# A new step table, norm moments partly on GpSimd, and a split key-value eviction in a one-core transformer block

## The chip, the core and the metric

The kernel runs on one core of a Trainium2 chip. A core has TensorE (PE, matmuls, with a separate weight load, PEld), VectorE (DVE), ScalarE (ACT), GpSimd (POOL) and SyncE (SP, which here only issues DMAs). Each engine works through its own queue in order; semaphores hold an instruction until what it needs is there. The metric is the device time of one execution in microseconds, lower is better.

## What is computed

S = 2048 tokens, D = 448, 16 heads of 28, Fh = 896. All inputs are bf16.

```python
mod = silu(c) @ w_mod                       # six rows sa, ca, ga, sb, cb, gb of 448
h = layernorm(x) * (1 + ca) + sa
q, k, v = split(h @ wqkv)                   # 16 heads of 28
phi(u) = concat(softmax(u @ w_phi), softmax(-(u @ w_phi)))     # 56 features a head
kv = phi(k)^T @ v;  z = sum_s phi(k)
x = x + ga * (((phi(q) @ kv) / (phi(q) @ z + 1e-6)) @ wo)
h = layernorm(x) * (1 + cb) + sb
z = gelu(h @ w_in);  z1, z2 = z[:, :896], layernorm(z[:, 896:])
g = w_sp @ z2 + b_sp[:, None]               # 2048 x 2048 over the tokens
out = x + gb * ((z1 * g) @ w_out)
```

## The kernel before, in words

The fast path does everything on 16 token tiles of 128. (A general path stands behind a flag that the fast path computes; it isn't taken with these inputs.) Its stages, with the names of the steps:

- *Head.* wq and wk are transposed on PE (FTq, FTk, two halves each), copied out of PSUM (ETq, ETk), multiplied with the block-diagonal w_phi (PFq, PFk, four pieces each) and copied out again (EPq, EPk). The first layer norm's shift and scale are folded into the weights: csA and ccA form the columns on PE, esA and ecA evict them, SHq, SHk, SHv put the shift in as one more row of the weights, SCq, SCk, SCv scale the rows. The first token tiles get their statistics (l1s, l1e, l1r), are normalised (l1a) and transposed on PE (X, copied by XE); the others are transposed by DMA (T1). Steps du are warm-up matmuls on zeros.
- *Key stage.* For each tile i: kM (keys), kE and kF (exponential of plus and minus on ACT), kS (sums, DVE), kR (reciprocal), kP (normalise, on DVE or POOL), vM, vC (values, copied by ACT), kA (accumulate kv over the tiles in one bank). qM, qE, qF make the query features in eight steps that take 1024 columns each.
- *Between.* gr and ge form the gates ga and gb, wos and wts multiply them into wo and wout. KV masks the accumulated kv into a block-diagonal table KVbd, and a second small step writes its column 28. csB, ccB, esB, ecB, SHw, SCw fold the second norm into w_in (f_win).
- *Attention out.* Per tile nM (numerators), nX and nC, per pair nS (denominators), per tile nT (weights the numerators, DVE, f_t), nA (adds the two halves, into f_opad), T2 (DMA transpose), wM or wN (times wo; wN also adds x through a matmul with the identity), wR (evicts the new x with its row sum; on ACT after wN, on DVE with the addition of x after wM), wQ (row sum of squares).
- *Second norm.* l2R (moments from the two sums, four small DVE instructions), l2r (power -0.5, POOL), l2a (normalise), T3 (DMA transpose into f_hT).
- *z stage.* Per tile zM and zG (second half, gelu with row sum), zQ (squares), zR, zW and zN as l2R, l2r and l2a. yM and yG (first half) for each of four groups of 512 tokens and seven column pieces.
- *Token mixing.* w_sp is loaded transposed in 32 pieces (W), eight for each of four 512-column parts; part 0 has its own tile, parts 1 and 2 take the place of the query features, part 3 that of f_hT. gM sums over the 16 tiles, gG adds b_sp (bsp) and multiplies with z1, oM multiplies with wout, oE adds x, oD stores.

PSUM is cut by hand into five slots: A0, A1, A2 of two banks, B0, B1 of one. A step with @A1 waits until the readers of the step that had A1 before are done. The order in which the engines get all this is a table written out in the program, ORDER (line 482 and on): a word is a step with its arguments, after a slash the engine where there is a choice (V DVE, S ACT, G POOL, Y SP), after @ the PSUM slot. The loop at line 1092 issues the words one after the other, so every engine's queue is the table with the other engines' words left out. DMAs are words too (ld, T1 to T3, W, oD), nearly all in SP's queue; an SP word whose tile isn't ready holds back the words after it.

A scaling with one factor for each row is, on every engine but ACT, one instruction with a single multiplication (line 764):

```python
eng.tensor_scalar(out=out_, in0=in_, scalar1=sc, scalar2=None, op0=ALU.mult)
```

Lines that the prediction uses: L753, L758 shift rows; L764 scaling; L785, L801 head matmuls; L789, L791 copies; L819 l1a; L842 kM; L850 vM; L856 kS; L863 kP; L873 kA; L879, L881 KV; L890 qM; L895 qE and qF; L918 nM; L934 nT; L948 identity matmul of wN; L950 wM; L955, L957 wR; L970 to L973 moments; L976 powers; L990 zM; L1012 zN; L1018 yM; L1026 W; L1034 gM; L1047 oM; L1050 oE.

Of the kernel before, what the change touches and what calls it, by code (L numbers as in the profile page):

```python
# [482 lines left out]
ld:c/S ld:x0/Y ld:wq/S ld:x1/Y tbl ld:phi/Y m1/V m2a/G du:1@A2 ld:wk/Y ct@B0 ld:x2/Y du:8@A2 m2b/G ce:1 l1s:0 ld:wsa/Y ld:wca/Y ce:2 m3 ce:3 ld:x3/Y  # L483
l1e:0,1/G ce:4 FTq:1@B1 ld:wv/Y m4 l1s:1 ld:x4/Y FTq:0@B0 ETq:1/S du:7@A2 ETq:0/V l1r:0,1 ld:x5/Y bd/V l1e:1,2/V PFq:2@B0 l1a:0/V l1r:1,2 PFq:3@B1
PFq:1@A2 EPq:2/S ld:wo/Y FTk:0@A1 EPq:3/V EPq:1/S l1a:1/V X:0@B0 W:0,0 FTk:1@B1 l1s:2 XE:0/S X:1@A2 l1s:3 ETk:1/S PFq:0@B0 ETk:0/V l1e:2,4/G EPq:0/S
csA@A0 XE:1/S l1r:2,4 PFk:2@B0 esA PFk:3@B1 ld:wsb/S SHq@A2 EPk:3/V l1a:3/G ccA@A1 l1a:2/G X:3@B1 ecA PFk:0@A0 EPk:2/V SCq:0/S PFk:1@A1 SCq:1/V XE:3/S
X:2@B0 EPk:0/V du:6@A2 EPk:1/S l1s:4 SCq:3/S SHk@B1 l1s:5 XE:2/S SCq:2/S SHv@A2 SCk:2/V l1s:6 SCk:1/S qM:0@A1 SCk:0/S SCv:2/V SCk:3/V SCv:1/S SCv:3/V
l1s:7 SCv:0/S kM:0@B0 l1s:8 l1e:4,8/G qF:0 vM:0@B1 l1s:9 l1r:4,8 kE:0 vM:1@A2 l1s:10 kF:0 l1a:4/G vC:0 vM:2@B0 kS:0 vC:1 l1a:5/G vM:3@B1 qE:0 l1a:7/V
T1:4,6 kM:1@A2 kR:0 vC:2 l1a:6/V kP:0/G vC:3 l1s:11 kM:2@A1 T1:6,8 kE:1 l1s:12 kM:3@B0 kF:1 kF:2 l1s:13 qM:1@A2 l1e:8,12/G W:0,1 kE:3 kS:1 kF:3
l1r:8,12 kE:2 l1s:14 kA:0@A0 l1a:11/G qF:1 qM:2@A1 kS:2 l1a:10/G qE:1 W:0,7 kR:1 l1a:9/G kS:3 vM:4@B0 qF:2 l1a:8/G T1:10,12 vM:5@B1 kR:2 l1s:15 vC:4  # L490
kM:4@A2 qE:2 kP:1/V T1:8,10 kM:5@B0 kP:2/V kF:4 kR:3 kA:1@A0 kE:4 ld:wout/Y l1e:12,16/V kP:3/V kM:6@A1 ld:bsp/S l1r:12,16 W:0,3 kS:4 kE:5 kM:7@A2 kF:5
vC:5 kA:2@A0 kS:5 l1a:12/G kM:8@B0 kE:6 l1a:14/G kR:4 kF:6 kA:3@A0 kR:5 kP:4/V l1a:13/G vM:6@B1 ld:wmgb/Y kF:7 kS:6 kE:7 kA:4@A0 vC:6 vM:7@A1 kP:5/G
T1:12,14 kS:7 kE:8 vM:8@B1 kF:8 kR:6 vC:7 vM:9@A2 kS:8 l1a:15/G vC:8 ld:wmga/Y kA:5@A0 kP:6/V T1:14,16 kM:9@B0 vC:9 kR:7 kR:8 kA:6@A0 kP:7/V kE:9
kM:10@B1 kF:9 kP:8/V kA:7@A0 kS:9 kE:10 kM:11@B0 kF:10 kA:8@A0 kR:9 kF:11 kS:10 kP:9/G vM:10@B1 kE:11 vM:11@A2 kS:11 vC:10 ld:win1/S kM:12@B0 ld:wcb/Y
kR:10 vC:11 kR:11 kA:9@A0 kP:10/V kE:12 kM:13@B1 kP:11/V kF:12 kA:10@A0 kS:12 kF:13 kM:14@B0 kE:13 kA:11@A0 kR:12 kF:14 kS:13 kP:12/G vM:12@B1 kE:14
vM:13@A2 kS:14 vC:12 kM:15@B0 vC:13 kR:13 kR:14 kA:12@A0 kP:13/V kE:15 vM:14@B1 kP:14/V kF:15 kA:13@A0 scb kS:15 vC:14 vM:15@B0 kA:14@A0 kR:15 vC:15
kP:15/V gr:0@B1 kA:15@A0 ge:0 gr:1@B0 KV:0 wos:0/G ccB@B1 ge:1 wos:1/V qM:3@A2 wos:2/G ecB KV:1 wos:3/G csB@B0 qF:3 nM:0@A1 esB nM:1@A0 wts:1/G nX:0
SHw:3@B0 nC:0 ld:win0/Y nX:1 qE:3 nC:1 SHw:2@B1 nS:0 qM:4@A2 SCw:0,3/V SCw:2,1/S SCw:3,1/G nT:0 SCw:1,1/S nT:1 nA:0/G qM:5@A1 SCw:0,2/S qE:4 nA:1/G
# [654 lines left out]
```

## Time and profile before

| what | value |
|---|---|
| three runs, median (lowest to highest) | 266.71 us (266.34 to 267.99) |
| the profiled execution, its time | 266.28 us |
| its span, first to last instruction | 264.4 us |
| mean granted TensorE clock | 0.991 |
| PE, DVE, ACT, POOL busy | 254.1, 159.1, 113.2, 67.6 us |
| first wide matmul (qM:0) | 17.9 us |
| end of the last kA, with both gr | 56.0 us |
| end of zM:0 | 83.7 us |
| first gM | 138.5 us |
| last eviction starts, ends | 260.3, 260.95 us |

The profile shows one execution. Times in it count from the span's first instruction. Some 1.9 us of the execution lie outside the span. The duration of an instruction is longer than the distance to the next one where two follow each other, since their ends overlap: two exponentials of 448 columns (0.56 us each by the mean) take 0.98 together.

### The profile page before, as it was taken

What the parts mean: (1) busy time and instruction counts of PE and PEld (TensorE: products, weight loads), DVE (VectorE), ACT (ScalarE), POOL (GpSimd) and SP (SyncE); (2) the same over time, 40 slices, a digit from 0 to 9 for tenths busy, and PEclk for the clock granted to TensorE, in tenths of its full rate; (3) what the DMA queues carried; (4) which work ended last, traced back from release to release, by engine and by line L of the source; (5) the groups of instructions that cost most, each with busy time, mean ns of one, the idle gap of its engine ahead of it and who ended that gap; (6) DMA issues with size and microseconds to landing.
All of it is one profiled execution on the core that took longest, in us unless ns stands there. A gap on an engine that the chain in (4) does not pass through costs nothing.

```text
span 264.4 us, 4350 instructions
## 1 busy us (share of the span) xinstructions
PE 254.1 (96%) x1632; PEld 138.3 (52%) x1640; DVE 159.1 (60%) x389; ACT 113.2 (43%) x238; POOL 67.6 (26%) x93
## 2 busy tenths in 40 slices
...
PEclk9999999999979999999999999999999999999999
...
GB/s 183 280 240 117 157 240 250 281 5 13 106 147 174 119 82 41 160 160 42 185 186 29 0 0 0 2 0 0 0 5 35 97 180 132 0 0 30 24 36 80
DMA packets 68656, 25.23 MB, mean 95 GB/s; under 512 B 58129, under 2 KB 68498, under 8 KB 68626
## 3 DMA queue, kind: packets, MB, share of 16 engines
...
q10 hardware_dynamic: 1538, 2.15, 3.7%
q8 instruction: 15, 0.25, 0.4%
...
## 4 chain that ended last, share of the span: by engine, by line
PE 90%; ACT 3%; DVE 3%; DMA 2%; issue 1%; ACTq 0%; DVEq 0%
PE g_ps L1034 37%; PE z_ps L990 9%; PE z_ps L1018 9%; PE o_ps L1047 8%; PE q_ps L890 5%; PE k_ps L842 4%; PE x_ps L950 4%; PE v_ps L850 4%; PE kvacc L873 3%; PE num L918 2%; DMA f_wq_raw<-in_A_wqkv_dram 2%; DVE f_t L934 1%; PE tps L785 1%; PE sh_ps L758 1%; ACT f_Wq L762 1%; PE pf_ps L801 1%
## 5 line engine op out<-in xcount | busy, mean ns | idle before, releaser
L1034 PEld LDWEIGHTS <-f_z2n 128*128 128x128 bf16 x560 | 50.4, 98 | 47.6
L1040 DVE TENSOR_TENSOR f_gb<-g_ps,f_bsp 128x512 f32<-128x512 f32 (+2 forms) x35 | 20.4, 583 | 58.9 <-PE g_ps L1034 58.7
L1034 PE MATMUL g_ps<-f_Eq,f_z2n 128*128 128x512 bf16 x219 | 48.7, 379 | 0.3
L1021 ACT ACTIVATE f_z1T<-z_ps 128x512 bf16<-128x512 f32 x28 | 16.2, 595 | 71.0 <-PE z_ps L1018 71.0
L1018 PE MATMUL z_ps<-f_hT,f_win 113*128 113x512 bf16 (+1 forms) x112 | 26.4, 379 | 0.0
L990 PE MATMUL z_ps<-f_win,f_hT 112*128 112x448 bf16 (+1 forms) x128 | 26.1, 352 | 0.0
L1034 PE MATMUL g_ps<-f_hT,f_z2n 128*128 128x384 bf16 (+1 forms) x224 | 25.4, 272 | 0.0
L1034 PE MATMUL g_ps<-f_wsp,f_z2n 128*128 128x512 bf16 x109 | 24.5, 379 | 0.2
L1047 PE MATMUL o_ps<-f_wout,f_z1T 128*128 128x448 bf16 x112 | 22.8, 353 | 0.0
L1041 DVE TENSOR_TENSOR f_z1T<-f_gb,f_z1T 128x512 bf16<-128x512 f32 (+2 forms) x35 | 20.5, 585 | 1.9 <-ACT f_z1T L1021 0.5
L990 PEld LDWEIGHTS <-f_hT 112*128 112x128 bf16 (+1 forms) x128 | 12.3, 97 | 11.8
L856 DVE TENSOR_REDUCE f_ksum<-f_E 128x32 f32<-128x896 bf16 x16 | 16.8, 1067 | 0.8 <-ACT f_E L845 0.7
L1050 DVE TENSOR_TENSOR f_xpad<-o_ps,f_x 128x448 bf16<-128x448 f32 x16 | 9.3, 620 | 13.0 <-PE o_ps L1047 12.5
L1018 PEld LDWEIGHTS <-f_win 113*128 113x128 bf16 (+1 forms) x112 | 10.7, 97 | 12.3
L895 ACT ACTIVATE f_Eq<-q_ps 112x1024 bf16<-112x1024 f32 x16 | 16.0, 1034 | 2.7 <-PE q_ps L890 2.7
L934 DVE TENSOR_TENSOR f_t<-num,f_w 128x896 bf16<-128x896 f32 x16 | 16.7, 1084 | 0.2
L994 ACT ACTIVATE f_z2g<-z_ps 128x896 bf16<-128x896 f32 x16 | 14.6, 914 | 3.6 <-PE z_ps L990 3.5
L845 ACT ACTIVATE f_E<-k_ps 128x448 bf16<-128x448 f32 x32 | 15.4, 556 | 1.6 <-PE k_ps L842 0.9
L1047 PEld LDWEIGHTS <-f_z1T 128*128 128x128 bf16 x112 | 10.7, 98 | 9.4
L950 PE MATMUL x_ps<-f_wo,f_oT 112*128 112x448 bf16 x64 | 15.2, 367 | 0.0
L890 PE MATMUL q_ps<-f_hT,f_Wq 113*128 113x512 bf16 (+1 forms) x64 | 14.9, 378 | 0.0
L842 PE MATMUL k_ps<-f_Wk,f_hT 113*128 113x448 bf16 (+1 forms) x64 | 14.1, 352 | 0.0
...
## 6 DMA issues: line engine op xcount, KB each, us to landing
...
```

The lines of the kernel that those rows point to most:

```text
L842: nc.tensor.matmul(t[:, 0, 0:D], lhsT=hT[0:KR[m], i, m, :], rhs=Wk[0:KR[m], m, :], start=(m == 0), stop=(m == KC - 1))
L856: nc.vector.tensor_reduce(out=ksum[:, i], in_=Er[i % NR][:].rearrange("p s (c f h) -> p (s c) h f", c=4, h=HP), axis=AX.X, op=ALU.add)
L890: nc.tensor.matmul(t[:, u, :], lhsT=Wq[0:KR[m], m, cc * CB:cc * CB + P], rhs=hT[0:KR[m], 4 * st:4 * st + 4, m, :], start=(m == 0), stop=(m ...
L934: nc.vector.tensor_tensor(out=tr[i % 2][:], in0=numv(i)[:, :, :, 0:DH], in1=wr[i // 2 % 2][:, i % 2].unsqueeze(3).to_broadcast([P, 2, H, D ...
L950: nc.tensor.matmul(t[:, 0, 0:D], lhsT=oT[0:CB, i % 4, cc, :], rhs=wo_s[0:CB, cc, :], start=(cc == 0 and not with_x), stop=(cc == KC - 1))
L990: nc.tensor.matmul(t[:, hf, 0:D], lhsT=hT[0:KR[m], i, m, :], rhs=win_s[0:KR[m], m, FH + hf * D:FH + (hf + 1) * D], start=(m == 0), stop=(m ...
L1018: nc.tensor.matmul(t[:, 0, :], lhsT=win_s[0:KR[m], m, fc * P:(fc + 1) * P], rhs=hT[0:KR[m], 4 * st:4 * st + 4, m, :], start=(m == 0), stop ...
L1021: nc.scalar.activation(out=stage_b()["z1T"][:, fc, st * 512:(st + 1) * 512], in_=ps["y%d_%d" % (st, fc)][:, 0, :], func=ACT.Gelu_apprx_tanh)
L1034: nc.tensor.matmul(g[:, 0, 0:b - a], lhsT=later["z2n"][:, s_, fc * P:(fc + 1) * P], rhs=wspT[t][:, s_, a:b], start=(s_ == 0), stop=(s_ == ...
L1040: nc.vector.tensor_tensor(out=gb, in0=ps["G%d_%d" % (ch, fc)][:, 0, 0:b - a], in1=bsp[:, t * TCHF + a:t * TCHF + b], op=ALU.add)
L1041: nc.vector.tensor_tensor(out=z, in0=gb, in1=z, op=ALU.mult)
L1047: nc.tensor.matmul(ps["o" + str(t)][:, 0, 0:D], lhsT=later["z1T"][:, fc, t * P:(t + 1) * P], rhs=wout_s[:, fc, :], start=(fc == 0), stop=( ...
```

## The change

There are five parts.

1. ORDER is another table: the same steps, but in another order, some on other engines and other PSUM slots. In numbers: wN stands 4 times instead of 9 (the others are wM); wR is on DVE 12 times instead of 7; kP on POOL 6 times instead of 4; l1a on POOL 14 times instead of 12; l2a on POOL 15 times instead of 7; zN on POOL 5 times instead of 3; SCw on POOL 5 times instead of 2 and on DVE no more; wts on DVE 5 times instead of 1; warm-up matmuls 20 instead of 22; loads on ACT's queue 3 instead of 5. Before the first gM stand 20 yM words (24 before) and 24 W words (17 before).
2. moments takes an engine. On POOL it is five instructions, on DVE four as before. Three of the eight l2R and four of the eight zR are on POOL.
3. A scaling on POOL adds 0.0 and then multiplies, in one instruction.
4. KV is split: the masking of one half stays on DVE, that of the other is four ACT copies with the mask's column as scale (a float copy of the mask is made at the start); the small step for column 28 is a word of its own, KZ, on DVE.
5. A step dm (small matmuls on zeros) is defined, and the table doesn't use it.

The diff of the functions:

```diff
+        nc.vector.tensor_copy(out=maskf[:], in_=mask[:])
...
     def scale_on(eng, out_, in_, sc):
         if eng is nc.scalar:
             nc.scalar.activation(out=out_, in_=in_, func=ACT.Copy, scale=sc)
+        elif eng is nc.gpsimd:
+            eng.tensor_scalar(out=out_, in0=in_, scalar1=0.0, scalar2=sc, op0=ALU.add, op1=ALU.mult)
...
-    def KV(s):
+    def KV(s, eng):
         kvv = ps["kv"][0:CB, s, 0:464].rearrange("p (c h d) -> p c h d", c=4, h=HP)
-        nc.vector.tensor_tensor(out=KVbd[0:CB, s, :, :, 0:29], in0=kvv,
-                                in1=mask[0:CB].unsqueeze(1).unsqueeze(3).to_broadcast([CB, 4, HP, 29]), op=ALU.mult)
+        if eng is nc.scalar:
+            for h in range(HP):
+                nc.scalar.activation(out=KVbd[0:CB, s, :, h, 0:29], in_=kvv[:, :, h, :], func=ACT.Copy, scale=maskf[0:CB, h:h + 1])
+        else:
+            nc.vector.tensor_tensor(out=KVbd[0:CB, s, :, :, 0:29], in0=kvv,
+                                    in1=mask[0:CB].unsqueeze(1).unsqueeze(3).to_broadcast([CB, 4, HP, 29]), op=ALU.mult)
+
+    def KZ(s):
+        kvv = ps["kv"][0:CB, s, 0:464].rearrange("p (c h d) -> p c h d", c=4, h=HP)
         nc.vector.scalar_tensor_tensor(out=KVbd[0:CB, s, :, :, 28], in0=kvv[:, :, :, 28], scalar=0.5e-6,
...
-    def moments(a, b, t1, t2, n, nm, v):
-        nc.vector.tensor_scalar(out=nm[:, a:b], in0=t1[:, a:b], scalar1=-1.0 / n, scalar2=None, op0=ALU.mult)
-        nc.vector.tensor_tensor(out=sq[:, a:b], in0=nm[:, a:b], in1=nm[:, a:b], op=ALU.mult)
-        nc.vector.scalar_tensor_tensor(out=v[:, a:b], in0=t2[:, a:b], scalar=1.0 / n, in1=sq[:, a:b], op0=ALU.mult, op1=ALU.subtract)
-        nc.vector.tensor_scalar(out=v[:, a:b], in0=v[:, a:b], scalar1=0.0, scalar2=LN_EPS, op0=ALU.max, op1=ALU.add)
+    def moments(a, b, eng, t1, t2, n, nm, v):
+        eng.tensor_scalar(out=nm[:, a:b], in0=t1[:, a:b], scalar1=-1.0 / n, scalar2=None, op0=ALU.mult)
+        eng.tensor_tensor(out=sq[:, a:b], in0=nm[:, a:b], in1=nm[:, a:b], op=ALU.mult)
+        if eng is nc.gpsimd:
+            eng.tensor_scalar(out=v[:, a:b], in0=t2[:, a:b], scalar1=1.0 / n, scalar2=None, op0=ALU.mult)
+            eng.tensor_tensor(out=v[:, a:b], in0=v[:, a:b], in1=sq[:, a:b], op=ALU.subtract)
+        else:
+            eng.scalar_tensor_tensor(out=v[:, a:b], in0=t2[:, a:b], scalar=1.0 / n, in1=sq[:, a:b], op0=ALU.mult, op1=ALU.subtract)
+        eng.tensor_scalar(out=v[:, a:b], in0=v[:, a:b], scalar1=0.0, scalar2=LN_EPS, op0=ALU.max, op1=ALU.add)
```

The old table where the prediction speaks of it: the head up to the first wide matmul, and the stretch in which PE stands still.

```text
ld:c/S ld:x0/Y ld:wq/S ld:x1/Y tbl ld:phi/Y m1/V m2a/G du:1@A2 ld:wk/Y ct@B0 ld:x2/Y du:8@A2 m2b/G ce:1 l1s:0 ld:wsa/Y ld:wca/Y ce:2 m3 ce:3 ld:x3/Y
l1e:0,1/G ce:4 FTq:1@B1 ld:wv/Y m4 l1s:1 ld:x4/Y FTq:0@B0 ETq:1/S du:7@A2 ETq:0/V l1r:0,1 ld:x5/Y bd/V l1e:1,2/V PFq:2@B0 l1a:0/V l1r:1,2 PFq:3@B1
...
l1s:7 SCv:0/S kM:0@B0 l1s:8 l1e:4,8/G qF:0 vM:0@B1 l1s:9 l1r:4,8 kE:0 vM:1@A2 l1s:10 kF:0 l1a:4/G vC:0 vM:2@B0 kS:0 vC:1 l1a:5/G vM:3@B1 qE:0 l1a:7/V
...
T2:0,1 qF:4 nM:2@A0 SHw:0@B0 T2:1,2 nX:2 qE:5 nC:2 nM:3@A2 wts:2/G SCw:0,0/V SHw:1@B1 nX:3 qF:5 nC:3 wN:0@B0 nS:1 SCw:1,0/G SCw:0,1/S nM:4@A1 nT:2
SCw:2,0/S wN:1@B1 nX:4 nT:3 SCw:3,0/S W:0,5 nM:5@A0 nA:2/G nX:5 wR:1/S nC:4 nC:5 nM:6@A2 nA:3/V nS:2 wR:0/S T2:2,4 wQ:1/S nT:4 nX:6 wQ:0/S nT:5
nM:7@A1 nA:4/G W:0,6 nX:7 nC:6 wN:2@B0 nC:7 nA:5/V nS:3 W:1,1 wN:3@B1 wR:2/S l2R:0,2 qM:6@A0 wR:3/S nT:6 T2:4,6 l2r:0,2 wQ:2/S l2a:0/G nT:7 qM:7@A2
```

The new table at the steps of the prediction: head, first T1, end of the key stage, attention out, z stage, end.

```text
m1/G m3 ld:c/S ld:x0/Y ld:wq/S du:1@A2 ct@B0 tbl ce:1 du:8@A2 FTq:0@B1 FTq:1@A2 m2a/V ce:2 ce:3 ce:4 m4 ld:x1/Y l1s:0 l1e:0,1/V l1s:1 scb l1r:0,1
l1a:0/V ETq:1/S du:3@A1 X:0@B0 l1e:1,2/G l1r:1,2 l1a:1/V XE:0/S ETq:0/S ld:wk/Y FTk:1@A1 FTk:0@A2 ETk:0/S ld:phi/Y ETk:1/V bd/V X:1@B0 du:4@A1
PFq:2@B1 EPq:2/S PFq:0@A1 EPq:0/S XE:1/V ld:x2/Y l1s:2 l1s:3 PFk:3@A2 PFq:3@B0 EPq:3/S l1e:2,4/G l1r:2,4 l1a:2/G l1a:3/G PFk:1@A0 PFk:2@B1 PFq:1@A1
EPq:1/S EPk:2/S EPk:1/S ld:wsa/Y csA@B0 PFk:0@A1 esA EPk:0/S EPk:3/V ld:wca/Y SHq@B0 ccA@B1 SHk@A2 ecA SCq:1/V SCk:3/V SCk:1/V SCk:2/V ld:x3/Y l1s:4
l1s:5 l1s:6 l1s:7 l1e:4,8/G l1r:4,8 l1a:4/G l1a:5/G X:2@B1 X:3@A1 l1a:7/G l1a:6/G SCq:3/S SCk:0/S XE:2/S XE:3/S SCq:0/S du:4@A2 kM:0@A2 kM:1@B1
kM:2@B0 kF:0 kE:0 SCq:2/S ld:wv/Y SHv@A2 kF:1 kF:2 ld:x4/Y ld:x5/Y W:0,7 ld:win0/Y T1:4,6 SCv:0/S SCv:1/S kE:1 qM:0@A1 kS:0 SCv:3/V kR:0 SCv:2/V
...
vC:14 kA:14@A0 vC:15 gr:1@B0 gr:0@B1 ge:1 kS:15 kR:15 kP:15/V kA:15@A0 wts:1/V KV:0/V wts:4/V KZ:0 ge:0 KV:1/S KZ:1 wos:2/V wts:3/V qM:3@A2 nM:0@A1
...
SCw:2,0/G qF:5 nM:6@A2 wR:0/S SCw:0,1/S wQ:0/S nX:6 wN:1@B0 wR:1/S nM:7@A1 nX:7 wQ:1/S l2R:0,2/G l2r:0,2 T2:2,4 W:0,1 W:0,4 wN:2@B1 wR:2/S wQ:2/S nC:6
nC:7 nS:3 nT:6 nT:7 T2:4,6 W:1,2 qM:6@A0 qE:6 qF:6 l2a:0/V wM:3@B0 qM:7@A2 wR:3/V nM:8@A1 nM:9@A0 wM:4@B0 wM:5@B1 qE:7 nX:8 qF:7 nX:9 nA:6/G nA:7/V
...
zM:8@A0 zM:9@A2 wQ:13/S wM:14@B0 wM:15@B1 zG:8 zG:9 yM:1,0@A0 yM:0,2@A2 yG:1,6 zR:6,8/V wQ:12/S l2R:12,14/V l2r:10,12 l2a:10/G l2a:11/G zQ:8/S zW:6,8
l2r:12,14 l2a:12/G l2a:13/G W:0,0 yG:1,0 yG:0,2 T3:10,12 zM:10@A1 zM:11@A2 zN:6/V zN:7/V zQ:9/V wR:15/V wR:14/V wQ:14/S wQ:15/S l2R:14,16/V T3:12,14
W:2,6 zR:8,10/G zW:8,10 zG:10 zG:11 zQ:11/S l2r:14,16 l2a:15/G l2a:14/G zN:8/V W:2,7 zN:9/V zQ:10/V zR:10,12/V zW:10,12 zN:10/V T3:14,16 W:2,1 W:1,5
yM:2,0@B0 zM:12@A1 zM:13@A2 zG:12 zG:13 zQ:13/S zQ:12/V zR:12,14/V W:2,3 W:1,3 W:2,5 zN:11/G zW:12,14 zN:12/V zN:13/G yM:1,4@B1 yM:1,3@A1 yG:1,3
yG:1,4 W:1,0 W:2,2 W:0,6 zM:14@A2 zM:15@A1 zG:14 zG:15 zQ:15/S W:1,6 W:2,0 W:1,1 ld:bsp/Y yM:3,4@B1 yM:3,2@A2 yM:2,4@A1 yM:0,4@A0 zQ:14/V zR:14,16/V
...
gG:1,0 guard@B0 yM:1,2@B0 yM:2,3@A1 oE:0 oE:1 oM:2,0,7@A2 oE:2 oM:3,0,7@A0 yG:2,3 yM:2,5@A2 gM:1,5@A1 W:3,5 W:3,2 oD:1/Y yG:1,2 oD:2/Y gG:1,1 gG:1,5
```

94 lines of the change are left out of this document (49 added, 45 removed).

## The prediction

> **What bounds the kernel now.** I read the page's busy shares and slices first, then the table of stretches, the chain of waits, the queue of SyncE (SP) in order of time, and last the groups by line for prices.
>
> ```profile
> PE 254.1 (96%) x1632; PEld 138.3 (52%) x1640; DVE 159.1 (60%) x389; ACT 113.2 (43%) x238; POOL 67.6 (26%) x93
> PEclk9999999999979999999999999999999999999999
> PE 90%; ACT 3%; DVE 3%; DMA 2%; issue 1%; ACTq 0%; DVEq 0%
> ```
>
> TensorE (PE) is busy nearly always and holds 90% of the chain. So a new order can gain only where PE isn't doing full-rate work. The third line of the page's slices, PEclk, dips once, in slice 12. The stretches show where (start:end, length, then busy time of PE, weight load, DVE, ACT, POOL, granted clock, DMA share, GB/s):
>
> ```profile
> 5.65:17.90 12.25, 11.59 (x138) 9.61 (x139) 8.28 (x24) 7.21 (x13) 3.26 (x6) 1.00 1.14 288
> 64.00:70.00 6.00, 5.78 (x56) 3.63 (x55) 4.40 (x11) 5.93 (x12) 6.00 (x5) 1.00 0.44 84
> 70.00:73.00 3.00, 1.05 (x15) 0.89 (x13) 2.83 (x7) 2.15 (x9) 0.65 (x2) 0.84 0.42 94
> 73.00:76.20 3.20, 3.20 (x15) 1.51 (x13) 2.83 (x12) 0.82 (x3) 1.02 (x2) 0.62 0.96 163
> 138.50:258.00 119.50, 119.08 (x670) 61.44 (x677) 49.52 (x88) 3.96 (x7) 1.70 (x2) 1.00 0.16 32
> ```
>
> From 138.5 on nothing is to be had: 119.08 of 119.50. The first 17.9 us look busy but hold 138 small matmuls and warm-up ones. At 70 to 73 PE stands still, and until 76.2 it runs at a granted clock of 0.62. The chain says on what (start, us, what):
>
> ```profile
> 65.58 0.68 DVE f_win L764
> ...
> 67.69 2.09 DVE f_t L934 x2
> ...
> 71.22 1.10 DVE f_t L934
> 72.32 0.05 issue
> 72.37 0.98 PE num L918 x8
> 73.35 0.37 PE x_ps L948
> 73.72 1.49 PE x_ps L950 x4
> 75.22 0.37 PE x_ps L948
> 75.58 0.76 PE x_ps L950 x4
> ```
>
> DVE's queue is behind there: the eviction of win (L764) stands ahead of the attention combine (f_t, 1.05 us each). Four x_ps matmuls then take 1.49 where they take 0.76 at full clock. Idle 2.2 plus slow matmuls 1.75 (0.56+0.73+0.18+0.18 and small change) make about 4.0 us lost.
>
> **The change part by part.** The profiled execution took 266.28 us (span 264.4; last matmul ends at 260.33); the median of the three runs is 266.71, 0.43 more, which I add at the end. Per step on PE, from the chain: four 448-wide matmuls 0.76, eight 512-wide ones 1.74, one kA or nM step 0.42.
>
> 1. *Head.* Before, the first wide matmul (qM:0) starts at 17.9, and at 28.2 PE has done qM:0, qM:1, kM:0-3, vM:0-3, kA:0. In the new table the ACT queue runs without a gap from wq's transposes (in at 5.65, done 7.39, as now): ETq:1, XE:0, ETq:0, ETk:0, then seven EP copies. In the old trace such copies start 0.80, 0.48, 0.80, 0.80 and 0.42 after each other, so 2.9 + 7 x 0.42 = 5.8, plus small waits: 13.4. SHk follows (0.9, to 14.5), three scalings on DVE at 0.3 (15.4), and kM:0 starts at 15.6. PE then needs 9.98 for the same steps plus SHv 0.75: 26.4 instead of 28.2. Gain 1.8. Bounds: if each of the 11 copies costs its row's mean (0.53 or 0.91) in place of its pace, 1.2 is lost and other ACT steps slip too, gain -0.5; if nothing waits at all, 2.9. I take 1.8, because the pace is what the old queue shows back to back.
> 2. *Key stage, to the last kA and both gate matmuls.* PE has 27.8 us of work (24 k/v steps x 0.76, 15 x 0.42, qM:2, gr), so 54.2 instead of 56.0 if it is fed. DVE from its first key sum at 18.4: 16 sums x 1.04, 16 reciprocals x 0.31, 10 kP x 0.58 (12 before; POOL takes 6 of 1.69, not 4), 8 statistics x 0.74, two scalings: 34.0, done at 52.4. kA:15 needs it at 53.7. No change, under 1.3 us of cover. T1's transposes now stand in SP's queue behind win0, then wo and wout: 1.2 MB at the 250 GB/s of the head is 4.7 us, and kM:8 comes 3 us after; free.
> 3. *Key-value halves.* Before: 0.64 + 0.23 twice on DVE. Now four ACT copies of 112x116 (between 0.18 for 32 wide and 0.53 for 448 wide; I take 0.25) beside DVE. Both lie under qM:3 (1.74); without that cover they'd be worth 0.5. Counted nothing.
> 4. *56 to the end of zM:0.* Before 27.7 us (56.0 to 83.69). PE's work there is 23.4. DVE per pair of tiles: 0.4 + 0.85 + 2.08 + 0.7 = 4.0, four pairs 16.1, and both win evictions (0.68) have gone to ACT, so DVE stays under PE's 18.6 for the same tiles. POOL's win scalings were a single multiply, 2.54 each; add and multiply on the same width is this row:
>
> ```profile
> L764 POOL TENSOR_SCALAR f_win<-f_win,f_cb 112x896 bf16<-112x896 bf16 x2 | 5.1, 2536 | 1.4 <-PE sh_ps L758 1.4
> L1012 POOL TENSOR_SCALAR f_z2n<-f_z2g,f_zm,f_zv 128x896 bf16<-128x896 bf16 x3 | 3.7, 1242 | 0.3
> ```
>
> Five at 1.24 are 6.2, done before zM:0 needs them. Following the queues by these durations, PE waits about 0.9 in all: 0.3 for esB before SHw:3, 0.1 for nT:1, 0.1 for qF:4, 0.2 for qF:5 before nM:6 and wR:0 behind it, 0.2 at qM:5 and nM:8. 24.3, so gain 3.4, of which 0.2 is one identity matmul: 3.2. Bounds 1.5 (half of the wait is back) and 4.0.
> 5. *Identity matmuls* (wN 9 to 4): 5 x 0.19 = 0.9 gain. Their wR go from ACT to DVE (0.62; 12 there, not 7).
> 6. *z stage.* ACT is the tight one: 16 zG x 0.91, 12 zQ x 1.05, wQ, wR, yG. It holds until zM:12, which needs zG:10, which stands behind wQ:14 and wQ:15, which wait for wR:14 on DVE, which waits behind l2R:12,14 for wQ:12: PE stands 1.4 us. Loss 1.4; bounds 0 and 3.0 (below).
> 7. *Moments on POOL.* Seven of sixteen, 35 POOL operations for 28 of DVE (0.16). Bounds: 0.24 (L812, POOL tensor_scalar) and 0.58 (the one-element power, L816): 1.2 to 2.9 against 0.7 per set. They are two columns wide and no power: I take 0.28. Three sets feed T3; only l2R:0,2 has no slack.
> 8. *Transposes.* T3:0,1 and T3:2,4 now follow a W piece in SP's queue and are needed at once. Landing is 2.8 for T and 3.9 for W pieces: 1.1 once; bounds 0 and 2.2.
> 9. *Guard.* yM:1,2 reuses the guard's bank behind a DVE step: 0.3.
> 10. *Loads and the end.* ACT issues three loads instead of five (0.33 to 0.42 each): 0.7 off ACT, none of it on PE. bsp moves to SP, behind eleven wsp pieces; it lands by 140 and the first gG reads it at 141; if it is late, PE has another gM (3.5) before it needs that bank. From the first gM on, each bank's reader has at least one step of 0.9 to 3.5 us as cover, the last outputs leave in the same order of evictions, and PE's steps are the same. Nothing. The wsp pieces are the third rival.
>
> Sum: 1.8 + 3.2 + 0.9 - 1.4 - 1.1 - 0.3 = 3.1. 266.28 - 3.1 + 0.43 = 263.6.
>
> **A rule against it.** Beside POOL work DVE's scaling of wo took 0.70 (that of wout, alone, 0.385), and in the order of time a DVE kP at 35.82 took 0.78 where two together at 31.01 took 1.13. [...] For step 6 the rows are the clock after 70 us: about 2 us of idling, then 0.62. [...]
>
> **Rivals.**
> - *The head gives nothing* (265.4): ACT's chain has no gap to absorb a late wk, wca or copy; the old one had 1.7 idle twice. 263.6 + 1.8.
> - *POOL is the bound* (270): it gets some 17 us more work. With 0.2 on each of ten kP and 2.06 for POOL's kP (both rows exist), kA:15 comes 1.3 late; moments at 0.58 put zM:0 2.2 late; in the z stage zM:12's wait grows by 3. Together 6.5. Slower than before from 3.1. Against: POOL stays idle for two thirds.
> - *wsp lands late* (268.8): 24 pieces, not 17, must be in before the first gM. Eight are issued behind T3:14,16 (115.4); nine took this:
>
> ```profile
> 125.75 12.11 SPq L1026 DMA_TRANSPOSE f_Eq<-in_B_w_sp_dram  x9
> ```
>
> 1.35 each, so the last needed lands at 124.8 + 4 = 129, and gM:0 comes at 130.6. At 1.55 a piece it begins to cost; at 2.2 (as the one at 75.91) it costs 8 x 0.85 - 1.6 = 5.2.
>
> **How the numbers follow.** Forecast 0.47; head gives nothing 0.31; POOL 0.14; wsp 0.08. A measurement of this kernel tells about 1% (2.7 us) from no change: under 264.0 is faster, over 269.4 slower. The forecast lies just inside faster; POOL and part of wsp are slower: 0.47, 0.33, 0.20. Low end: head 2.9, no wait at zM:12, no late transposes, less 0.9 for all at once not happening: 260.9. High end: 268.6, which leaves out most of the POOL case and the top of wsp. The forecast's own range is 261.5 to 265.
>
> **What would show it.** First k_ps matmul near 15.6; last kvacc near 54; no PE wait on f_t and a clock of 1.0 from 64 to 77; first z_ps (L990 before) near 77; a PE wait on ACT for z_ps near 112; win scalings on POOL near 1.24; last matmul near 257. Wrong if k_ps starts after 17.5, if POOL's small operations exceed 0.5, or if PE waits for a transpose or for wsp.

## The result, and the profile after

The changed kernel takes 268.78 us (median of 10 runs, 267.98 to 269.26) where the kernel before takes 266.68 (10 runs beside it): ratio 1.0072, 95% interval 1.0052 to 1.0093. It is slower, by 2.1 us. The forecast was 263.6, with a range to 268.6: the sign was wrong, and the time lies just outside the range. The profiled execution took 269.01 us, with a span of 267.1 (264.4 before).

The page after: busy shares, the granted clock by slices, the chain by engine.

```profile
PE 253.5 (95%) x1625; PEld 137.1 (51%) x1633; DVE 159.9 (60%) x365; ACT 109.5 (41%) x227; POOL 87.5 (33%) x139
...
PEclk9999999999999999999999999999999999999999
...
PE 77%; DVE 8%; DMA 4%; POOL 3%; ACT 3%; issue 2%; ACTq 0%; POOLq 0%; DVEq 0%
```

The dip of the clock is gone, and POOL has 20 us more work. But PE holds only 77% of the chain instead of 90%: DVE, DMA and POOL now end waits on the path. The same stretches as before (start:end, length, busy time of PE, weight load, DVE, ACT, POOL, clock, DMA share, GB/s):

```profile
5.65:17.90 12.25, 11.75 (x135) 9.76 (x135) 7.33 (x21) 9.04 (x16) 3.97 (x9) 1.00 1.13 292
64.00:70.00 6.00, 5.51 (x50) 3.32 (x49) 5.57 (x13) 4.82 (x8) 3.03 (x3) 1.00 0.22 44
70.00:73.00 3.00, 3.00 (x25) 1.75 (x23) 2.41 (x8) 3.00 (x10) 1.07 (x2) 1.00 0.50 97
73.00:76.20 3.20, 3.10 (x23) 1.55 (x21) 3.06 (x9) 2.82 (x12) 2.65 (x7) 1.00 1.09 185
138.50:258.00 119.50, 118.89 (x668) 61.16 (x674) 47.50 (x83) 4.36 (x8) 0.00 (x0) 1.00 0.15 30
```

At 70 to 76.2, where PE had 1.05 of 3.00 us and then a clock of 0.62, it now has 6.10 of 6.20 at full clock. That repair came as forecast. Where the rest went is seen in PE's own waits (who waits for whom: us in total, times, longest):

```profile
PE z_ps L1009 <- DMA f_hT<-f_xpad: 2.1, 3, 0.8
PE kvacc L877 <- DVE f_phik L867: 1.3, 1, 1.3
...
PE num L929 <- DVE f_KVbd L892: 0.7, 1, 0.7
PE x_ps L965 <- DMA f_oT<-f_opad: 0.5, 1, 0.5
PE num L929 <- DVE f_t L949: 0.4, 1, 0.4
...
PE z_ps L1037 <- DVE flag L1081: 0.2, 1, 0.2
```

None of the first four existed before. By stage, from the ends of the same steps in both traces (us):

| stage | before | after | forecast | measured |
|---|---|---|---|---|
| to the state with qM:0,1, kM:0-3, vM:0-3, kA:0 done | 28.23 | 28.11 | -1.8 | -0.1 |
| to the last kA, both gr done | 27.78 | 29.33 | 0 | +1.6 |
| to the end of zM:0 | 27.68 | 25.50 | -3.2 | -2.2 |
| to the end of the last matmul | 176.61 | 179.64 | +1.9 | +3.0 |
| to the end of the span | 4.06 | 4.55 | 0 | +0.5 |
| sum | 264.4 | 267.1 | -3.1 | +2.8 |

(The fourth row's +1.9 is the forecast's 1.4 + 1.1 + 0.3 less 0.9 for the identity matmuls. Nearly all of its 3.0 is idle time of PE: 3.2 us in this stretch after, 0.4 before.) One group shows the price on which the third stage hung, POOL's scaling of win, 2536 ns each before:

```profile
L766 POOL TENSOR_SCALAR f_win<-f_win,f_cb 112x896 bf16<-112x896 bf16 x5 | 5.6, 1128 | 4.6 <-PE sh_ps L760 2.6 <-issue 2.0
```

### The profile page after: what moved, and what is told of

Same layout as the page of the kernel before. It is cut to its first block, busy times and chain, and to the rows that moved or that the text cites. A ratio compares the mean times of both kernels' runs of the same rounds, so it can differ in the third digit from the quotient of the medians.

```text
span 267.1 us, 4338 instructions
## 1 busy us (share of the span) xinstructions
PE 253.5 (95%) x1625; PEld 137.1 (51%) x1633; DVE 159.9 (60%) x365; ACT 109.5 (41%) x227; POOL 87.5 (33%) x139
## 4 chain that ended last, share of the span: by engine, by line
PE 77%; DVE 8%; DMA 4%; POOL 3%; ACT 3%; issue 2%; ACTq 0%; POOLq 0%; DVEq 0%
PE g_ps L1053 36%; PE o_ps L1066 8%; PE z_ps L1037 7%; PE k_ps L846 5%; PE v_ps L854 4%; PE z_ps L1009 3%; PE q_ps L901 3%; PE kvacc L877 3%; PE x_ps L965 2%; DMA f_wq_raw<-in_A_wqkv_dram 2%; DMA f_oT<-f_opad 2%; DMA f_hT<-f_xpad 1%; PE num L929 1%; DVE f_x L972 1%; PE tps L789 1%
## 5 line engine op out<-in xcount | busy, mean ns | idle before, releaser
L1040 ACT ACTIVATE f_z1T<-z_ps 128x512 bf16<-128x512 f32 x28 | 15.2, 599 | 42.0 <-PE z_ps L1037 41.9
L1053 PE MATMUL g_ps<-f_hT,f_z2n 128*128 128x384 bf16 (+1 forms) x224 | 24.8, 272 | 0.0
L1037 PEld LDWEIGHTS <-f_win 113*128 113x128 bf16 (+1 forms) x112 | 10.8, 97 | 12.9 <-issue 0.2
L949 DVE TENSOR_TENSOR f_t<-num,f_w 128x896 bf16<-128x896 f32 x16 | 16.8, 1085 | 0.3
L965 PE MATMUL x_ps<-f_wo,f_oT 112*128 112x448 bf16 x64 | 13.9, 353 | 0.6 <-DMA f_oT<-f_opad 0.5
```

The lines of the kernel that those rows point to most:

```text
L949: nc.vector.tensor_tensor(out=tr[i % 2][:], in0=numv(i)[:, :, :, 0:DH], in1=wr[i // 2 % 2][:, i % 2].unsqueeze(3).to_broadcast([P, 2, H, D ...
L965: nc.tensor.matmul(t[:, 0, 0:D], lhsT=oT[0:CB, i % 4, cc, :], rhs=wo_s[0:CB, cc, :], start=(cc == 0 and not with_x), stop=(cc == KC - 1))
L1037: nc.tensor.matmul(t[:, 0, :], lhsT=win_s[0:KR[m], m, fc * P:(fc + 1) * P], rhs=hT[0:KR[m], 4 * st:4 * st + 4, m, :], start=(m == 0), stop ...
L1053: nc.tensor.matmul(g[:, 0, 0:b - a], lhsT=later["z2n"][:, s_, fc * P:(fc + 1) * P], rhs=wspT[t][:, s_, a:b], start=(s_ == 0), stop=(s_ == ...
```

## The experiments

Each ratio is to the kernel before, run beside it on the same chip. Times of kernels that ran on different chips are not compared directly, but by these ratios; 0.0010 is 0.27 us.

| run | what | us | ratio (95%) |
|---|---|---|---|
| | the change | 268.78 | 1.0072 (1.0052 to 1.0093) |
| a_kp_order | kP:8 ahead of kR:9 | 267.58 | 1.0032 (1.0015 to 1.0048) |
| a_kv_dve | both halves on DVE | 267.55 | 1.0038 (1.0018 to 1.0058) |
| a_maskf_last | one tile's place | 268.96 | 1.0099 (1.0062 to 1.0136) |
| b_shift32 | before, tiles 32 bytes on | 268.05 | 1.0047 (1.0016 to 1.0077) |
| c_three | the first three together | 266.38 | 0.9994 (0.9972 to 1.0015) |
| a_mom_dve | moments back on DVE | 274.09 | 1.0282 (1.0249 to 1.0315) |
| b_mom | before, moments on POOL | 266.76 | 0.9999 (0.9980 to 1.0018) |
| a_scale_one | POOL scales by one multiply | 272.26 | 1.0212 (1.0180 to 1.0245) |
| b_win | before, with win's scalings | 267.78 | 1.0049 (1.0025 to 1.0073) |
| a_nodu3 | the change, less warm-up | 268.41 | 1.0053 (1.0034 to 1.0072) |
| d_nodu | c_three, last warm-up group out | 266.70 | 1.0004 (0.9976 to 1.0031) |
| e_nodu3 | c_three, three groups out | 265.14 | 0.9961 (0.9938 to 0.9983) |
| b_nodu | before, less warm-up | 270.02 | 1.0115 (1.0094 to 1.0135) |
| c_three_w | c_three, one W piece later | 267.19 | 1.0011 (0.9990 to 1.0032) |
| d_best | c_three, two W later, l2a on DVE | 266.76 | 1.0006 (0.9981 to 1.0032) |
| e_fill | c_three, PE's order in the z stage | 265.83 | 0.9986 (0.9963 to 1.0010) |
| e_nosq | c_three, four squares on DVE over 64 columns, not 896 | 265.37 | 0.9980 (0.9958 to 1.0002) |
| g_best | e_nodu3 and e_fill | 266.36 | 1.0000 (0.9977 to 1.0023) |

### Key stage: the engines shut each other out

```diff
-kR:9 kR:8 kP:8/V kP:9/G
+kR:8 kP:8/V kR:9 kP:9/G
```

> The changed kernel with kP:8 put ahead of kR:9, so that POOL's kP:9, which needs kR:9, can't start until DVE's kP:8 is over. The same instructions on the same engines. Theory (the two engines lock each other out): DVE's kP:8 took 2.02 us because POOL's kP:9 (1.69) had started 0.15 before it; now it takes 0.62, PE's wait of 1.33 us for it is under 0.3, and the time falls by 1.0 to 1.5 to 267.3 to 267.8. Rival (the wait is DVE's load or the order of the table): kP:8 is short too, but PE waits as long for a later product, kP:9 on POOL being 0.6 later, and the time stays within 0.3 of 268.8.

The stretch in the changed kernel, in order of time (start, us, engine, line, what; idle time before it and what ended it):

```profile
42.28 0.30 DVE L864 RECIPROCAL f_kr<-f_ksum 128x32 bf16<-128x32 f32 x1
...
42.53 1.69 POOL L867 TENSOR_TENSOR f_phik<-f_E,f_kr 128x896 bf16<-128x896 bf16 x1 [0.56 <-DVE f_kr L864]
...
42.68 2.02 DVE L867 TENSOR_TENSOR f_phik<-f_E,f_kr 128x896 bf16<-128x896 bf16 x1
...
44.76 0.43 PE L877 MATMUL kvacc<-f_vaug,f_phik 128*128 128x116 bf16 x5 [1.33 <-DVE f_phik L867]
```

and with the two words swapped:

```profile
42.14 0.63 DVE L867 TENSOR_TENSOR f_phik<-f_E,f_kr 128x896 bf16<-128x896 bf16 x1
...
43.20 1.69 POOL L867 TENSOR_TENSOR f_phik<-f_E,f_kr 128x896 bf16<-128x896 bf16 x1 [1.11 <-ACT f_vaug L857]
...
44.95 0.59 PE L877 MATMUL kvacc<-f_vaug,f_phik 128*128 128x116 bf16 x8 [0.23 <-POOL f_phik L867]
```

Same instructions, same engines. In the first fence DVE's product starts 0.15 us after POOL's and ends 0.48 after it, as if it got going only when POOL was through. In the second it takes 0.63; the next product on DVE, started at 44.47 and so 0.42 before POOL's end, takes 0.90 and again ends 0.48 after it. PE's wait falls from 1.33 to 0.23, and the ratio falls by 0.0040, about 1.1 us, with intervals that don't meet. The theory holds; its rival, a wait that comes back later in the stage, took back 0.23.

### The key-value halves

```diff
-KV:0/V wts:4/V KZ:0 ge:0 KV:1/S KZ:1
+KV:0/V wts:4/V KZ:0 ge:0 KV:1/V KZ:1
```

> The changed kernel with the second key-value half on DVE again (one operation of 0.64 in place of four ACT copies, in the same place). Theory: the split costs, because ACT's copies waited 1.05 us for DVE's KZ:0 and ended at 59.75, while DVE alone ends all four steps at about 59.2; PE's wait of 0.69 for f_KVbd is under 0.2, and the time falls by 0.5 to 0.8 to 268.0 to 268.3. Rival (DVE is the tight engine behind it): the attention combine comes 0.64 later, PE's wait for f_t at 64.9 grows from 0.42 to about 1.0, and the time stays at 268.8.

The changed kernel:

```profile
57.47 0.64 DVE L887 TENSOR_TENSOR f_KVbd<-kvacc,f_mask 112x464 bf16<-112x464 f32 x1 [0.21 <-PE kvacc L877]
...
58.33 0.22 DVE L892 SCALAR_TENSOR_TENSOR f_KVbd<-kvacc,f_mask 112x16 bf16<-112x16 f32 x1
...
58.64 1.11 ACT L885 ACTIVATE f_KVbd<-kvacc,f_maskf 112x116 bf16<-112x116 f32 x4 [1.05 <-DVE f_KVbd L892]
...
60.07 0.32 PE L929 MATMUL num<-f_KVbd,f_Eq 112*128 112x120 bf16 x3 [0.69 <-DVE f_KVbd L892]
```

ACT's copies wait for DVE's column step of the other half: the two are not beside each other but one behind the other, and a third step waits for ACT. On DVE alone the last column step starts at 58.80 instead of 59.79 (0.3 of that is an earlier end of the key stage in this execution), PE doesn't wait, and the kernel is 1.2 us faster by the medians, 0.9 by the ratios (the intervals just meet); the rival's price, more waiting for f_t, did not appear (0.38 where it was 0.42).

### The 32 bytes

The float mask is a 16-byte tile in the middle of the long-lived ones. It moves all that come after it. By the author's working from the tiles' sizes, f_xpad and f_opad, from which the DMA transposes read, lay at 79616 and 87808 and now lie 32 bytes on; the traces show no addresses.

```diff
     mask = persist.tile([P, HP], BF, name="f_mask")
-    maskf = persist.tile([P, HP], F32, name="f_maskf")
     KVbd = persist.tile([P, 2, 4, HP, 30], BF, name="f_KVbd")
...
     oT = persist.tile([P, 4, KC, P], BF, name="f_oT")
+    maskf = persist.tile([P, HP], F32, name="f_maskf")
```

> The changed kernel with one line moved: the 16-byte tile f_maskf is allocated behind f_oT instead of ahead of f_KVbd, so that f_xpad and f_opad lie at 79616 and 87808 again (multiples of 256, as before) and not 32 bytes further. No instruction changes. Theory (the address): every two-tile transpose out of f_xpad and f_opad lands in 2.7 to 2.9 us as before, not in 3.7 to 3.9; the three waits of PE for f_hT (0.63, 0.79, 0.67 us, and some 0.15 each of weight load behind them) and the two for f_oT (0.1, 0.48) go, together 3.4 us of start-to-start time, of which other waits take back up to 1: 265.4 to 266.8. Rival (the queue: transposes are slower since the new order puts more transposes next to each other): landings stay at 3.7, and the time at 268.8.

And the kernel before with an unused tile there:

```diff
     mask = persist.tile([P, HP], BF, name="f_mask")
+    gapt = persist.tile([P, HP], F32, name="f_gap")
```

> The kernel before, with an unused 16-byte tile allocated where the change has f_maskf, so that f_xpad and f_opad move by 32 bytes. No instruction changes. Theory (the address): its two-tile transposes land in 3.7 to 3.9 us instead of 2.75. Each has some slack there (PE waited for none of them), so the time rises by 0 to 2 us: 266.7 to 268.7. Rival (the queue order of the change): landings stay at 2.75 and the time at 266.7.

DMA issues, median us from issue to landing at the end of the line; before, after, after with the tile moved, before with the shift:

```profile
f_hT<-f_xpad SPq DMA_TRANSPOSE x15, 2.8
...
f_oT<-f_opad SPq DMA_TRANSPOSE x9, 2.8
```

```profile
f_hT<-f_xpad SPq DMA_TRANSPOSE x15, 3.8
...
f_oT<-f_opad SPq DMA_TRANSPOSE x9, 3.8
```

```profile
f_hT<-f_xpad SPq DMA_TRANSPOSE x15, 3.1
...
f_oT<-f_opad SPq DMA_TRANSPOSE x9, 2.7
```

```profile
f_hT<-f_xpad SPq DMA_TRANSPOSE x15, 3.4
...
f_oT<-f_opad SPq DMA_TRANSPOSE x9, 3.2
```

The address counts in both directions, with no instruction changed: by these medians a transpose lands in 2.7 to 3.1 us from the old place and in 3.2 to 3.8 from the new one, 0.4 to 0.6 later in the kernel before and 0.7 to 1.1 in the changed one. The target f_hT is allocated ahead of the tile and does not move, so for T3 it is the source's place that counts. Why it counts, and which other places would do the same, these runs don't show. In the kernel before it costs 1.3 us (PE waits 0.58 for f_hT at 28.1 and 0.47 for f_oT at 73.9). But giving it back to the changed kernel gains nothing: PE's waits for transposes fall from 2.7 to 2.1 us only, with a new one of 1.28 for f_oT at 109, behind a W piece. As a cause of the 2.1 us the address alone fell.

> The changed kernel with three of the edits together: f_maskf allocated behind f_oT, kP:8 ahead of kR:9, the second key-value half on DVE. Alone they took +0.2, -1.2 and -1.2 us off 268.78. Theory (the losses of the key stage and of the halves are separate in time and add up; the late transposes cost little by themselves because the work behind them then waits for something else): 268.8 - 2.4 = 266.4, within 0.5, the transposes 2.75 long and PE still waiting some 2 us in the z stage. Rival (the transposes were the bound of the z stage once the rest is out of the way): 2 us less, 264.4. Rival (a later stage takes back what the earlier ones gain): 267.6 or more.

Measured 266.38: the losses of the key stage and of the halves add up, and with them undone the changed kernel is level with the one before. In its trace the last kA ends at 56.30 instead of 57.44, and zM:0 starts at 78.86 instead of 81.25.

### What the parts are worth

Moments back on DVE (all /G of l2R and zR to /V), and on POOL in the old table (l2R from tiles 0, 4, 6, zR from 0, 2, 4, 8):

> The changed kernel with its seven POOL sets of moments back on DVE, in the same places (28 DVE operations of 0.16 instead of 35 POOL ones of 0.22). Theory (DVE is the tight engine of the z stage, busy 14.17 of 15.00 us from 100 to 115, so that moving small work to POOL helps or costs nothing): 0.3 to 2 slower, 269.1 to 270.8. Rival (POOL's small operations cost DVE more by locking it out, and their longer chain, 1.05 instead of 0.7 us per set, delays the transposes): 0.4 to 1.5 faster, 267.3 to 268.4.

> The kernel before, with the same seven sets of moments on POOL that the change puts there. Nothing else. In the changed kernel taking them back to DVE cost 5.3 us. Theory (what moments on POOL are worth depends on the table: this one keeps PE fed in the z stage, with no wait there, so DVE's 4.6 us freed buy nothing, while each set is 0.35 us longer): -0.5 to +1.0, 266.2 to 267.7. Rival (freeing DVE is worth the same in any table): 2 us faster or more.

POOL's scaling as one multiply again, and win's scalings alone in the old table:

```diff
-            eng.tensor_scalar(out=out_, in0=in_, scalar1=0.0, scalar2=sc, op0=ALU.add, op1=ALU.mult)
+            eng.tensor_scalar(out=out_, in0=in_, scalar1=sc, scalar2=None, op0=ALU.mult)
```

> The changed kernel with POOL's scalings of win written as one multiply again (2.54 us each before, 1.01 alone with add and multiply). Theory (the add and multiply form is what makes five of them on POOL affordable): five take 12.7 us instead of 5.6, POOL's nA:6, l2a and T2:6,8 behind them come 2 to 4 us late, and the time rises by 1 to 4 to 270 to 273; DVE's statistics behind them are locked out for longer. Rival (POOL has slack there): within 0.4 of 268.8.

```diff
-SCw:0,3/V ... SCw:2,1/S ... SCw:0,0/V ... SCw:2,0/S ... SCw:3,0/S
+SCw:0,3/S ... SCw:2,1/G ... SCw:0,0/S ... SCw:2,0/G ... SCw:3,0/G
```

> The kernel before, its table unchanged but for the scaling of win: POOL scales by add and multiply, takes three of the four halves that ACT had (SCw:2,1, SCw:2,0, SCw:3,0), and ACT takes DVE's two evictions (SCw:0,3, SCw:0,0). Nothing else of the change. Theory (the wait of PE at 70 to 72.4 and the slow clock to 76 come from DVE's and ACT's share of this work, and the scaling is where the change's gain lies): DVE is 1.4 us and ACT 1.7 us freer before 70, the wait of 2.2 us falls under 1, the clock stays at 1.0, and the time falls by 1.5 to 4 to 262.7 to 265.2, below both kernels. Rival (the wait moves: nX behind qE on ACT, or POOL locks DVE out as it did for 0.3 us at 67.06): within 0.7 of 266.7.

By the ratios, in the new table the moments on POOL are worth 5.6 us and the scaling 3.7; in the old one the moments are worth nothing, and win's scalings cost 1.3. Undone, the scaling reads

```profile
L766 POOL TENSOR_SCALAR f_win<-f_win,f_cb 112x896 bf16<-112x896 bf16 x5 | 13.3, 2663 | 2.0 <-issue 2.0
```

and PE waits 1.46 for f_x (L972) at 80.5 and 1.55 for f_oT at 85.5. In b_win PE waits for f_t for 2.9 us, not 2.2. Beside POOL's three scalings (from 66.08 to 69.08) two DVE steps that f_t hangs on took 0.70 and 0.60 where they take 0.18 and 0.23 later: the 0.9 us lost there (0.3 in the kernel before) takes back part of what DVE gained, as the rival had it, though the time rose by more than its 0.7. So b_win doesn't tell order from price. a_scale_one does: without the cheap scaling the new table's wait for f_t is still 0.4, and the loss comes elsewhere. The order and the choice of engines removed the old stall; without either price cut the new table loses 4 to 6 us in other places. The theory of b_win fell, those of the other three held, a_mom_dve with a price well above the 2 us expected.

### The head

Steps du are warm-up matmuls. The new table has three groups of them behind wq's transposes, in PE's queue.

```diff
-du:3@A1 X:0@B0 ... du:4@A1 PFq:2@B1 ... du:4@A2 kM:0@A2
+X:0@B0 ... PFq:2@B1 ... kM:0@A2
```

> The kernel with three edits (266.4), without the four warm-up matmuls that stand between the transposes and the first key projection (they started at 16.57 after 0.34 us of waiting for ACT's SCk:0, and the first key matmul at 17.22). The output does not depend on them. Theory (the head's last link is the scaling of the key weights, done at 16.6, and the warm-up matmuls only add to it): the first key matmul starts at 16.7 and the time falls by 0.3 to 0.6 to 265.8 to 266.1. Rival (the clock needs them, or the state is set by qM:0, which waits for weights that are 1 us later): no change, or slower with a clock under 1.0 near 17.

> The kernel with three edits (266.4), without the three groups of warm-up matmuls (3, 4 and 4) that stand between the transposes and projections of the head. The output doesn't depend on them. Theory (ScalarE's chain of copies sets the head: its first product copy waited 0.72 us at 11.43 for projections that stood behind one such group): the first copy starts at 11.0, the first key matmul at 16.2 instead of 16.9, and the time falls by 0.4 to 0.8. Rival (VectorE's shift factors and the copies behind them are set by the loads): the first key matmul stays at 16.6, as without the last group alone. Without warm-up the granted clock may fall below 1.0 before 17; then it is slower by up to 1.

> The changed kernel without its three later groups of warm-up matmuls (3, 4 and 4 in the head), nothing else. Theory (they stand in PE's queue ahead of the projections that ScalarE's copies wait for; from the end of the wait for wq to the first key matmul the changed kernel takes 11.75 us, without them 9.82): 1.2 to 1.8 faster than 268.8, 267.0 to 267.6. Rival (the gain of the run with three edits was a matter of that kernel's loads): under 0.5.

> The kernel before without its two later groups of warm-up matmuls (7 and 6 in the head), nothing else. Theory (its ScalarE waits 1.7 us twice in the head, the first time for projections behind BD on VectorE, so PE's warm-up work fills time that is idle anyway): within 0.5 of 266.6. Rival (PE's queue is the head's chain here too): 1 to 2 faster, 264.6 to 265.6, and then the change's head is worth nothing by itself.

ACT and PE in the changed kernel (one fence for each), then PE in the run with three edits and no later warm-up:

```profile
11.43 1.95 ACT L793 CAST f_Wq<-pf_ps 112x448 bf16<-112x448 f32 x4 [0.72 <-PE pf_ps L805]
```

```profile
9.99 1.06 PE L706 MATMUL warm_ps<-f_zero 128*128 128x256 bf16 x4
10.85 0.76 PE L805 MATMUL pf_ps<-f_BD,f_wTq 112*112 112x112 bf16 x8
...
16.56 0.60 PE L706 MATMUL warm_ps<-f_zero 128*128 128x256 bf16 x4 [0.34 <-ACT f_Wk L764]
17.22 0.73 PE L846 MATMUL k_ps<-f_Wk,f_hT 113*128 113x448 bf16 x3
```

```profile
15.95 1.30 PE L846 MATMUL k_ps<-f_Wk,f_hT 113*128 113x448 bf16 x6 [0.34 <-ACT f_Wk L764]
```

ACT's first product copy waits 0.72 us for projections that stand behind four warm-up matmuls. From the first transpose of wq to the first key matmul the changed kernel takes 11.75 us (5.47 to 17.22). That is the slow end: eleven kernels with this head and all three groups took 10.8 to 11.8, with PE's rate in it (the four warm-up matmuls that take 1.06 above take 0.60 in d_best). Without the three groups it is 9.83, 9.86 and 10.28 in three kernels. The last group alone holds the first key matmul up by 0.65 (16.58 to 17.23 in c_three), and taking it out made no difference in time.

By the ratios the three are worth 0.9 us in the kernel with three edits (0.9994 to 0.9961; the intervals overlap) and 0.5, not the 1.2 to 1.8 expected, in the changed kernel itself (they overlap there too): in its profiled execution the first key matmul is 0.91 earlier, the last kA ends 0.64 earlier, and the first z matmul starts 0.13 earlier. Most is gone before the z stage begins.

The kernel before needs its warm-up: without it, it is some 3 us slower, which neither its theory nor its rival forecast. There PE is idle for 1.25 us ahead of the projections, and the shift rows that follow run at half rate, though the granted clock stands at 1.00. That accounts for 1.5 us, by the end of kA:0; the rest comes later (PE waits 1.34 for ACT until 83.8 and 1.78 for f_hT until 125.6) and is not explained. The shift rows, first without, then with the warm-up:

```profile
14.09 1.70 PE L753 MATMUL sh_ps<-f_Wq,f_Ga 112*128 112x448 bf16 x4
```

```profile
13.36 0.92 PE L753 MATMUL sh_ps<-f_Wq,f_Ga 112*128 112x448 bf16 x4
```

### The z stage, left open

PE waits three times for f_hT in the changed kernel; POOL's normalisation ahead of the last one takes 2.42 us for two (0.71 each alone):

```profile
117.10 2.42 POOL L998 TENSOR_SCALAR f_xpad<-f_x,f_m,f_v 128x448 bf16<-128x448 bf16 x2
...
117.73 3.22 PE L1009 MATMUL z_ps<-f_win,f_hT 113*128 113x448 bf16 x16 [0.79 <-DMA f_hT<-f_xpad]
...
119.54 1.23 SPq L1003 DMA_TRANSPOSE f_hT<-f_xpad  x1
...
120.83 9.68 SPq L1045 DMA_TRANSPOSE f_Eq<-in_B_w_sp_dram  x7
...
123.35 3.22 PE L1009 MATMUL z_ps<-f_win,f_hT 113*128 113x448 bf16 x16 [0.67 <-DMA f_hT<-f_xpad]
```

Five kernels tried to take such waits out of c_three. SP's order:

```diff
-T3:8,10 W:2,4 T2:14,16
+T3:8,10 T2:14,16 W:2,4
```

> The kernel with those three edits, and the W piece W:2,4 put behind T2:14,16 in SyncE's queue instead of ahead of it. In the run with f_maskf moved alone, T2:14,16, issued 1.8 us behind that piece, landed in 3.99 where others took 2.7, and PE waited 1.28 us for it at 109. Theory (a W piece just ahead makes a transpose late, and PE has no slack there): the landing falls to about 2.75, that wait goes, and the time is 1.0 to 1.3 below that of the three edits alone. Rival (the transpose waits for VectorE's nA:15, not for the queue; the work behind is bound by DVE): less than 0.4.

The wait for f_oT went (that transpose landed in 2.77), and one of 2.03 for T3:10,12 came, now behind two pieces, and brought the clock to 0.50 behind it: 1.0011. With both pieces behind T3:10,12, and l2a:14,15 on DVE:

> The kernel with three edits (f_maskf moved, kP:8 ahead, second half on DVE; 266.4), and two more: the W pieces W:2,4 and W:0,0 both behind T3:10,12 in SyncE's queue (with W:2,4 alone moved back, the two stood together ahead of T3:10,12, and PE waited 2.03 us for it), and l2a:14 and l2a:15 on DVE (0.39 each) in place of POOL, where the first took 1.71 beside DVE's zN. Theory (what is left of PE's waits in the z stage, 0.86, 1.08 and 0.52 in that kernel, comes from pieces just ahead of a transpose and from POOL waiting for DVE): the last two go, 1.2 to 1.7 faster, 264.7 to 265.2. Rival (DVE is full there, and 0.8 us more of it delays zQ and the moments behind): within 0.5 of 266.4.

T3:14,16 then was issued 2 us earlier, landed in 5.12, behind two pieces, and PE waited 1.39 at the same place (the profile names ACT's f_z1T, which ended within 0.02 us of the landing): 1.0006. PE's order instead (yM:1,0 ahead of wM:14, yM:0,4 ahead of zM:14, T3:2,4 ahead of W:1,4), and the squares of zQ on DVE over 64 columns, which leaves work out:

> The kernel with three edits (266.4), with PE's order changed at three places where it waited for a transpose (1.08 us for f_oT at 106.7, 0.52 and 0.86 for f_hT at 119.9 and 84.5): yM:1,0 goes ahead of wM:14, yM:0,4 ahead of zM:14, and in SyncE's queue T3:2,4 goes ahead of the piece W:1,4. The work of every engine is the same. Theory (the waits are landings that PE has no cover for, and a yM of 0.87 covers one): each of the three falls under 0.3, and the time by 1.2 to 2 to 264.4 to 265.2, below both kernels. Rival (VectorE's work bounds the stage, so PE waits as long a step later): within 0.5 of 266.4.

> The kernel with three edits (266.4), with its four squares of z on VectorE (zQ:9, 10, 12, 14; 1.08 us each) taken over 64 columns instead of 896, so that the moments of these tiles are not the reference's. That leaves 3.6 us of VectorE's work out between 110 and 130. Theory (landings without cover): VectorE's freed time lets T3:14,16 go at most 0.5 us earlier; 0 to 0.6 faster, 265.8 to 266.4. Rival (VectorE's work bounds the stage; 4.6 us more of it cost 5.3 in the run with all moments on it): PE's waits after 105 go, 1.2 to 1.7 faster, 264.7 to 265.2.

By the ratios, 0.9986 and 0.9980, they are 0.2 and 0.4 us faster than c_three, both inside its interval: e_fill's rival held, and e_nosq fits its theory, that the waits are landings without cover. In e_fill the three waits became 0.45 (for f_t), 0.79 (for ACT's gelu) and 0.41; in e_nosq PE still waited 0.71 and 0.70 after 105.

> The changed kernel with the edits that gained: f_maskf moved, kP:8 ahead of kR:9, second half on DVE, no later warm-up matmuls, and the three changes of order in the z stage. Alone and together they stood at 266.4 (three), 265.1 (three and no warm-up), 265.8 (three and the order). Theory (the gains lie in different stages and add up): 264.3 to 264.9, below both kernels by more than 1.5. Rival (the order in the z stage was within the noise): 265.1.

Both e_nodu3's head and e_fill's order gave 1.0000, not below 0.996; PE waited 1.61 for T3:14,16, which landed in 4.51. So e_nodu3 is the only kernel whose interval lies below 1, by 0.2 to 0.6%; as one of nineteen, and with g_best, which has the same head, at 1.0000, its gain is not secured. In every try 1.4 to 2.5 us of waits in the z stage were left, behind one releaser or another.

## Why the prediction failed, by its steps

Between 3.1 us faster and 2.8 slower lie 5.9 us: 1.7 in step 1, 1.6 in step 2, 1.0 in steps 3 and 4, 1.1 in steps 5 to 9, and 0.5 behind the last matmul. That the kernel is slower, and not merely less fast, hangs on steps 2 and 3: with these two undone and the tile moved (c_three) it is level.

- *Step 1, head, 1.8 expected, 0.1 measured.* "The ACT queue runs without a gap" failed. It needed 9.95 us from wq's arrival to the first key matmul; without the later warm-up matmuls that took 9.83 to 10.28, with them 11.75 here and 10.8 to 11.8 in eleven kernels. The sum of ACT's copies was right; the step left out what stands in PE's queue ahead of the matmuls that feed ACT, 1.0 to 1.9 us. And it took for granted that what the head gains reaches the end: a_nodu3 showed 0.5, inside the noise.
- *Step 2, key stage, 0 expected, 1.6 lost.* The sum of DVE (34.0) and its cover (1.3) stood on a kP of 0.58 each. One took 2.02 beside POOL. The term was in the text as the second rival, but spread as 0.2 on each of ten; it came as 1.40 on one, made PE idle for 1.33, which is all of PE's idle time in this stage, and the swap of two words takes back about 1.1 us.
- *Step 3, halves, 0 expected, 0.9 to 1.2 lost.* The copies cost what was taken (1.11 for four), but "beside DVE" failed: they ran behind it.
- *Step 4, to zM:0, 3.2 gained expected, 2.2 measured with step 3's wait of 0.7 inside.* Right in mechanism and nearly in size: clock 1.00, no stall, one wait of 0.42 for f_t; PE was busy for 24.2 us where 23.4 were taken. The price of the scaling (1.24 taken, 1.01 when nothing held it) carries it, as a_scale_one shows. That win's evictions on DVE made the old stall is not borne out: b_win took them off DVE, and the stall stayed.
- *Step 5.* Four identity matmuls took 0.76 us of PE instead of 2.08 for nine (some of those at the slow clock), 1.3 for 0.9: right.
- *Steps 6 and 8, 2.5 lost expected (1.4 + 1.1).* 2.1 of waiting for T3 and 0.5 for T2: the sum agrees by luck. The 1.4 on ACT at zM:12 through wR:14 was the wrong wait, and its upper bound of 3.0 an estimate that no run shows: PE's longest wait in this stage was 0.79, at a granted clock of 1.00. The late landing was taken once, and PE waited four times, for transposes that had become longer by up to 1.0 (medians of 3.8 us, 2.8 before). Undoing that did not bring the time back, since other landings then came late: why these waits stay is open.
- *Step 7.* POOL's small operations took 0.19 to 0.25 where DVE left them alone, 0.28 taken: right. Beside DVE some took up to 0.62. What they buy in this table, 5.6 us, was not seen.
- *Step 9.* 0.24 for 0.3: right. *Step 10:* no wait for W pieces or bsp, as forecast; 0.5 more after the last matmul is not explained.
- *The rivals.* "POOL is the bound" had the mechanism and the sign, at another place and price. wsp did not come late.
